# A memory-augmented block on one core: the late queries and keys move from the memory rows' softmax to the token rows' softmax

## The chip, the cores and the metric

One core of a Trainium2 chip runs the whole program. The metric is the device time of one execution in microseconds (us); of several runs the median is given.

## The reference

Input `x` is 2048 tokens of 512 numbers in bf16. The first half is a recurrent attention with 32 heads of 128, over 64 segments of 32 tokens, with 8 memory rows that go from segment to segment:

```
xn = layernorm(x); mem = mem0
for s in 64 segments:
    h = concat(mem (8 rows), xn[segment s] (32 rows))        # 40 rows
    q, k, v = h @ Wq, h @ Wk, h @ Wv
    scores = q k^T / sqrt(128); a token row sees the memory rows and the tokens up to itself,
                                a memory row sees all 40
    o = softmax(scores) v, then @ Wo
    mem = o[:8];  out[segment s] = o[8:]
h  = x + out
h2 = h + w2(gelu(w1 layernorm(layernorm(h)) + b1)) + b2
```

The mask is `(idx_q < 8) | (idx_q >= idx_k)`: a memory row (query index below 8) sees all 40 keys; a token sees the memory rows and the tokens up to and with itself. The memory rows of one segment are input to the projections of the next, so the segments form a chain.

## The kernel before

All weights lie in SBUF. The loop has 64 steps, one per segment (`s`); four segments form a block (`bk = s // 4`, `sg = s % 4`). The 40 rows of a segment are split into two packs. The first holds 24 tokens ("early" tokens) and the 8 memory rows and is projected in its own step, because of the memory rows (`hT`). The last 8 tokens of a segment ("late" tokens) depend on no memory row; those of four segments make 32 rows (`hB`) that are projected a block ahead: K in a step with sg = 0, Q with sg = 1, V with sg = 2 (parts `F0`, `F1`). With sg = 3 the same place holds the output product of the late rows (`wo_B`).

PE works in tiles of 128 rows by 32 columns: four matmuls side by side, 512 columns each, make a *pass unit*, and a projection of 16 heads has four (one per quarter of the 512 inputs). A unit that uses the same quarter of the same tokens as the unit just before it keeps the loaded tokens and issues no weight loads (`matmul_kept`, L604).

The parts of a step, in PE's order:
- `Q0`, `Q1`, `K0`, `K1` (L871): projections of 16 heads each. The result is copied by ACT or DVE (`kq`), transposed by DVE (L912) into `QT`, `KALL`, and the memory rows' queries are copied on into `ZC` by POOL (`ZCm`, L926).
- `SC0`, `SC1` (L1036): scores of the memory rows, for 16 heads each. `ZC` holds, per head, the 8 memory queries and the 8 late queries (`ZCb`, L933, POOL), so the stationary 32 columns are two heads with 16 rows each, and the scores are two groups of 64 keys (32 of the own pack and 32 of late keys, of which a mask leaves 8). The softmax `sc_softmax` is a maximum (L1044), two exponentials with sums (L1053, ACT), two reciprocals (L1058), two products (L1061) and one transposition to `PTC` (L1063, DVE).
- `V0`, `V1`: projections of V (`VS`).
- `PV0`, `PV1` (L1074, L1079): `PTC` times V, in tiles of 64 rows by 128 columns; L1079 takes the late values `VBD`. Out come the memory rows (`OTm`) and the late rows (`OTB`).
- `PVA` (L1142): the same for the token rows of the step before, from `BD`.
- `WO` (L1170): output product, eight units. Its result is transposed (`TT`, L1182) and summed into the next step's memory rows (`hTm`, L1176).
- `SA` (L1104): scores of the 24 token rows, 32 matmuls of 32 columns (32 keys; the late tokens' queries are not among them). Its softmax: L1114, L1115, L1116, L1117, L1118, the product `PA` (L1125), the transposition `PTA` (L1127), and four copies into the block form `BD` (L1131, POOL), which the next step's PVA reads.

The order on PE is written out by hand in four lists, one for each sg (`ORDERS`); an entry `('F1', 1, 2)` takes the part's units from 1 up to but not including 2. The other engines' orders come from a planner in the program: each operation has a duration and a planned time (`PLAN`, us), operations that more than one engine can do (`either`) go where they end first or where `HOME` says, and gaps are filled. After that `align()` counts PE's instructions in blocks of 256 and pads the pass units with up to 8 spare weight loads each (L869), so that a step of sg = 0, 1, 2, 3 begins at instruction 0, 64, 128, 192 of a block; if the stream is less than 24 instructions past that place nothing is done, else it is filled up to the next one:

```
owed = (PHASE[seg % 4] - at) % FETCH_N       # PHASE = (0, 64, 128, 192), FETCH_N = 256
if owed > FETCH_N - SLIP: owed = 0           # SLIP = 24
o.pad[0] = min(owed, PADS)                   # PADS = 8
```

After the loop comes a feed-forward phase (L1569, L1576) that the change leaves as it is.

## Time and profile before

| | us |
|---|---|
| median of 3 runs (lowest to highest) | 819.95 (818.89 to 820.13) |
| span of the profiled execution, first to last instruction | 817.0 |
| steps 1 to 3 begin at | 51.12, 63.03, 73.42 |
| steps 5 to 56 (94.74 to 637.48) | 542.74 |
| loop's end and feed-forward phase, from 730.31 | 86.7 |

The span leaves out 2.95 us of the median: what lies ahead of the first and behind the last instruction, and the difference between executions. In rows of a timeline the first number is the start in us from the span's start, the second the length; matmuls overlap, so PE is read from start to start. In rows of groups the last part is: busy time, mean ns of one | idle time of the engine just before them and what ended it.

### The profile page before, as it was taken

The page shows a single profiled execution, that of the slowest core. Times are in us where ns is not written, and L with a number is a line of the kernel's source. Part 1 is how long each engine was busy: PE and PEld are TensorE (multiplying, and loading weights), DVE is VectorE, ACT ScalarE, POOL GpSimd, SP SyncE. Part 2 cuts the span into 40 slices and gives each one's busy share as a digit, 9 for nine tenths or more (in the row PEclk, how much of TensorE's full clock was granted, in tenths as well). Part 3 has the DMA queues.
Part 4 walks back from the last instruction along what each step waited for, and adds up shares of the span by engine and source line. Part 5 has one row for each costly group of instructions (what it writes and reads, how often), then busy time and mean ns, then how long its engine had stood idle before and what let it go on. Part 6 is the DMA issues. An engine that isn't in the chain of part 4 may idle for free.

```text
span 817.0 us, 43604 instructions
## 1 busy us (share of the span) xinstructions
PE 780.8 (96%) x19317; PEld 426.6 (52%) x18878; DVE 622.1 (76%) x2008; ACT 529.6 (65%) x1522; POOL 351.2 (43%) x886
## 2 busy tenths in 40 slices
PE   3788999999999999999999999999999999999998
PEld 1345555555556555555555556555555555544443
DVE  3268797989898989898989898888899887833211
ACT  2446677767776767777777777767676766643442
POOL 5023334545454545454545454545463535367200
PEclk9989999999999999999999999999999999999999
DMA  8950010111101010101010201010112131265200
GB/s 341 391 173 16 4 25 15 30 30 27 32 21 39 17 42 14 45 10 43 10 49 10 49 10 49 10 49 3 49 29 62 37 91 26 76 173 147 55 26 26
DMA packets 65449, 48.03 MB, mean 59 GB/s; under 512 B 29028, under 2 KB 61676, under 8 KB 65260
## 3 DMA queue, kind: packets, MB, share of 16 engines
q1 hardware_dynamic: 64928, 44.98, 18.5%
q8 instruction: 150, 2.46, 1.3%
q14 instruction: 39, 0.32, 0.1%
q10 hardware_dynamic: 332, 0.27, 0.1%
HBM read 31.08 MB, written 8.13 MB: 48 GB/s over the span
## 4 chain that ended last, share of the span: by engine, by line
PE 77%; DVE 8%; ACT 7%; SPq 5%; issue 1%; DMA 1%; DVEq 0%
PE ps L871 33%; PE ps L1170 15%; PE quad L1576 6%; PE ps L604 5%; PE ps L1569 5%; ACT EC L1053 4%; PE quad L1074 4%; ACT kq L889 3%; DVE KALL L912 3%; SPq L791 2%; PE ps L1209 2%; DVE PC L1061 2%; SPq L774 2%; PE ps L1104 2%; DVE nmc L1044 2%; PE quad L1142 2%
## 5 line engine op out<-in xcount | busy, mean ns | idle before, releaser
L871 PE MATMUL ps<-WQ,hT 128*32 128x512 bf16 x2048 | 159.9, 384 | 5.7 <-DVE hT L1176 5.6
L1170 PE MATMUL ps<-WO,OT 128*32 128x256 bf16 x4224 | 141.3, 274 | 1.4 <-DMA WO<-in_A_Wo_dram 0.9
L871 PE MATMUL ps<-WV,hT 128*32 128x512 bf16 x1780 | 142.5, 379 | 0.0
L890 ACT ACTIVATE kq<-ps 128x512 bf16<-128x512 f32 x146 | 87.2, 597 | 66.1 <-PE ps L871 65.8
L1125 POOL TENSOR_TENSOR PA<-SA,rsa 128x256 bf16<-128x256 f32 x64 | 39.8, 621 | 187.4 <-DVE rsa L1118 174.5
L889 ACT CAST kq<-ps 128x512 bf16<-128x512 f32 x160 | 93.4, 583 | 37.8 <-PE ps L871 37.8
L1170 PEld LDWEIGHTS ps<-WO,OT 128*32 128x32 bf16 x4224 | 96.4, 96 | 24.4 <-issue 2.9
L1131 POOL COPY BD<-PTA 32x192 bf16<-32x192 bf16 x256 | 96.4, 376 | 16.7 <-DVE PTA L1127 0.9
L1061 DVE SCALAR_TENSOR_TENSOR PC<-EC,rsc,even 128x128 bf16<-128x128 f32 x256 | 94.6, 371 | 6.6
L871 PE MATMUL ps<-WK,hT 128*32 128x512 bf16 x1292 | 93.6, 379 | 0.0
L871 PEld LDWEIGHTS ps<-WQ,hT 128*32 128x32 bf16 x2048 | 60.5, 96 | 59.8 <-issue 19.4
L912 DVE STREAM_TRANSPOSE KALL<-kq 128x256 f32<-128x256 f32 x160 | 70.5, 441 | 22.9 <-ACT kq L889 20.6
L1053 ACT ACTIVATE EC<-quad,nmc 128x64 f32<-128x64 f32 x252 | 77.1, 311 | 7.6 <-DVE nmc L1044 0.9
L604 PE MATMUL ps<-WK,hT 128*32 128x512 bf16 x756 | 76.5, 382 | 0.0
L889 ACT CAST VS<-ps 128x512 bf16<-128x512 f32 x126 | 73.8, 586 | 0.9
L889 ACT CAST OT<-quad 128x128 bf16<-128x128 f32 (+1 forms) x193 | 65.2, 358 | 10.7 <-PE quad L1079 7.7
L912 DVE STREAM_TRANSPOSE QT<-kq 128x256 f32<-128x256 f32 x128 | 57.0, 446 | 18.7 <-ACT kq L890 18.6
L871 PEld LDWEIGHTS ps<-WV,hT 128*32 128x32 bf16 x1780 | 51.9, 96 | 33.7 <-issue 1.4
L1572 ACT ACTIVATE WQ<-ps,b1t 128x512 bf16<-128x512 f32 x42 | 28.9, 688 | 51.9 <-PE ps L1569 51.9
L1116 ACT ACTIVATE SA<-SA 128x256 f32<-128x256 f32 x64 | 26.7, 417 | 55.0 <-DVE SA L1115 52.7
L871 PEld LDWEIGHTS ps<-WK,hT 128*32 128x32 bf16 x1292 | 38.5, 97 | 44.5 <-issue 19.6
L1222 POOL TENSOR_TENSOR opT<-TTB,TTS 32x64 bf16<-32x64 f32 x128 | 40.3, 315 | 32.4 <-DVE opT L1176 23.2
(160 smaller groups left out, 1485.9 us busy)
## 6 DMA issues: line engine op xcount, KB each, us to landing
WV<-in_A_Wv_dram SPq DMA_DIRECT2D x4, 1024.0 KB, 10.4
WK<-in_A_Wk_dram SPq DMA_DIRECT2D x4, 1024.0 KB, 18.0
WQ<-in_A_Wq_dram SPq DMA_DIRECT2D x4, 1024.0 KB, 18.9
WO<-in_A_Wo_dram SPq DMA_DIRECT2D x16, 256.0 KB, 7.8
v_last<-VSB SPq DMA_DIRECT2D x60, 64.0 KB, 3.1
VBD<-v_last SPq DMA_DIRECT2D x60, 64.0 KB, 2.9
h_mid<-xr SPq DMA_DIRECT2D x16, 128.0 KB, 1.9
WQ<-h_mid SPq DMA_DIRECT2D x4, 512.0 KB, 4.3
```

What stands on the lines that cost most here:

```text
L604: return e.add_instruction(mybir.InstMatmult(name="I-%d" % (4000000 + _kept[0]), engine=mybir.EngineType.PE, start_tensor_calc=start, stop ...
L871: ins = e.matmul(o, l, m, start=(k == 0), stop=(k == DC - 1), tile_position=(0, 32 * j), skip_group_check=True)
L889: return {"act": (lambda e: e.copy(out, src), t_act(n, ps_)), "dve": (lambda e: e.tensor_copy(out, src), 0.155 + 1.0e-3 * n * fast)}
L890: return {"act": (lambda e: e.mul(out, src, scale_), t_act(n, ps_)), "dve": (lambda e: e.tensor_scalar(out, src, scale_, None, ALU.mult), ...
L912: S.op("dve", lambda e: e.transpose(out, src), reads=[("kq", i)], writes=[key], dur=t_dve(256) + 0.02)
L1053: return e.activation(EC[:, r, sl, :], o[:, sl, :], ACTF.Exp, bias=nmc[:, r, sl:sl + 1], accum_out=smc[:, r, sl:sl + 1])
L1061: S.op("dve", lambda e, sl=sl, xc=xc: e.scalar_tensor_tensor(PC[:, r, :, :, sl], xc, rsc[:, r, sl:sl + 1], ev, ALU.mult, ALU.mult), reads= ...
L1131: S.narrow(S.op("pool", lambda e, j=j, rows=rows: e.tensor_copy(BD[rows, par, :, j, :, :], PTA[rows, :, 0:NA, :]), reads=["PTA"], writes=[ ...
L1170: ins = e.matmul(ps[bank][32 * j:32 * j + 32, 0:256], lhs(slot(h)), wo_cols(h, b), start=(k == 0), stop=(k == 15), tile_position=(0, 32 * ...
L1222: return e.tensor_tensor(o[32 * q:32 * q + 32, c:c + 2], x, y, ALU.add)
L1569: ins = e.matmul(ps[bank][:, 0:SBT], W1[:, cc, fc * P:(fc + 1) * P], hnT_of(k)[:, cc, :], start=(cc == 0), stop=(cc == DC - 1))
L1576: S.op("pe", lambda e: e.matmul(quad[:, t, :], gT_of(k, fc)[:, t * P:(t + 1) * P], W2[:, fc, :], start=(fc == 0), stop=(fc == FC - 1)), re ...
```

## The change

The softmax of the memory rows keeps only the memory queries: `ZC` has 8 rows per head, the stationary 32 columns are four heads, and one group of 64 scores per SC remains. One maximum, one exponential, one reciprocal, one product per SC. The mask moves from `[128]` to `[64]` columns; PV has 16 columns per matmul and 64 for the late values.

The late queries go to SA: `ql_fill` writes them over the memory rows of `QT` after `ZCm` has been copied out, and `kl_fill` puts the segment's 8 late keys beside the 32 of the pack in `KALL` (`LK = 40` keys). SA then has 32 query rows and 40 keys. Its softmax grows from 8 x 32 to 8 x 40 numbers. A second product `PL` puts the late keys' weights into a fifth slice of `PA`; after the transposition a new product `BDL` (with a mask `maskD`) makes the block form for the late values. PVA gets 32 rows per head in place of 24 and four matmuls more, with `VBD`. `OTB` is copied out of PVA's result and no longer out of PV's. `ZCb` (`qb_fill`) is gone.

Besides, `ORDERS`, `PLAN`, `HOME` are new, and some durations that the planner uses; a hop from an engine to PE counts 0.06 more. The core of the diff:

```diff
-ORDERS = ((('Q0', 0, 1), ('K0', 0, 1), ('Q0', 1, 2), ('K0', 1, 2), ('Q0', 2, 3), ('Q1', 0, 1), ('Q0', 3, 4), ('K0', 2, 4), ('Q1', 1, 4), ('K1', 0, 4), ('SC0', 0, 99), ('V0', 0, 1), ('V1', 0, 1), ('V0', 1, 4), ('F1', 0, 1), ('SC1', 0, 99), ('V1', 1, 2), ('F0', 0, 1), ('V1', 2, 3), ('F1', 1, 2), ('V1', 3, 4), ('PV0', 0, 99), ('PVA', 0, 99), ('F1', 2, 3), ('WO', 0, 2), ('PV1', 0, 99), ('WO', 2, 8), ('F1', 3, 4), ('SA', 0, 99), ('F0', 1, 4)),
+ORDERS = ((('K0', 0, 2), ('Q0', 0, 2), ('K0', 2, 3), ('Q0', 2, 4), ('Q1', 0, 1), ('K0', 3, 4), ('Q1', 1, 4), ('K1', 0, 4), ('SC0', 0, 99), ('F0', 0, 1), ('V0', 0, 2), ('V1', 0, 1), ('V0', 2, 4), ('F1', 0, 1), ('SC1', 0, 99), ('V1', 1, 3), ('F1', 1, 2), ('V1', 3, 4), ('PV0', 0, 99), ('PVA', 0, 99), ('F1', 2, 3), ('WO', 0, 2), ('PV1', 0, 99), ('WO', 2, 8), ('F1', 3, 4), ('SA', 0, 99), ('F0', 1, 4)),
+          (('Q0', 0, 2), ('K0', 0, 1), ('Q0', 2, 4), ('K0', 1, 2), ('Q1', 0, 1), ('K0', 2, 4), ('Q1', 1, 4), ('K1', 0, 4), ('V0', 0, 1), ('SC0', 0, 99), ('V0', 1, 3), ('V1', 0, 1), ('V0', 3, 4), ('F1', 0, 1), ('SC1', 0, 99), ('V1', 1, 4), ('F1', 1, 3), ('PV0', 0, 99), ('PVA', 0, 99), ('F1', 3, 4), ('PV1', 0, 99), ('WO', 0, 8), ('F0', 0, 1), ('SA', 0, 99), ('F0', 1, 4)),
...
-        "SP0": (-1.81, -1.81, -1.52, -1.65),
+        "SP0": (-0.304, -1.667, 0.575, 1.283),
...
-        return HOP[p.eng]
+        return HOP[p.eng] + (0.06 if o.eng == "pe" else 0.0)
...
-        def qb_fill(s, after=()):
-            ...
-            S.op("pool", lambda e: e.tensor_copy(dst, src), reads=[("QTB", bk % 2, q) for q in range(2)], writes=[("ZCb", par)], dur=0.41, after=after)
+        def ql_fill(s):
+            ...
+            S.either({"act": (lambda e: e.copy(dst, src), 0.34), "dve": (lambda e: e.tensor_copy(dst, src), 0.24), "pool": (lambda e: e.tensor_copy(dst, src), 0.34)},
+                     reads=[("QTB", bk % 2, q) for q in range(2)], writes=[("QL", 0), ("QT", 0), ("QT", 1)])
+        def kl_fill(s):
+            ...
+                     reads=[("KB", bk % 2, q) for q in range(2)], writes=[("KL", s % 2)])
...
+            S.op("act", lambda e: e.activation(EC[:, r, :], o, ACTF.Exp, bias=nmc[:, r:r + 1], accum_out=smc[:, r:r + 1]),
+                 reads=[("nmc", r), bkey], writes=[("EC", r), ("smc", r)], dur=0.42)
+            S.op("dve", lambda e: e.reciprocal(rsc[:, r:r + 1], smc[:, r:r + 1]), reads=[("smc", r)], writes=[("rsc", r)], dur=0.16)
...
-            S.op("pe", f, reads=[("QT", 0), ("QT", 1), ("KA", par, 0), ("KA", par, 1)], writes=[("ps", bank)], dur=0.25, mode=MC, ni=64)
+            S.op("pe", f, reads=[("QT", 0), ("QT", 1), ("KA", par, 0), ("KA", par, 1), ("KL", par)],
+                 writes=[("ps", bank)], dur=0.26, mode=MC, ni=64)
...
+            S.either({k: (..., w) for k, w in (("dve", 0.24), ("pool", 0.32))}, ["SA", "rsa"], ["PL"], after=after)
...
-                S.narrow(S.op("pool", lambda e, j=j, rows=rows: e.tensor_copy(BD[rows, par, :, j, :, :], PTA[rows, :, 0:NA, :]), ...
+                S.narrow(S.op("pool", lambda e, j=j, rows=rows: e.tensor_copy(words(BD[rows, par, :, j, :, :]), words(PTA[rows, 0:4])), ...
+            S.either({k: ((lambda e: e.tensor_tensor(BDL[:, par], src, msk, ALU.mult)), w) for k, w in (("dve", 0.3), ("pool", 0.45))},
+                     reads=["PTA", "maskD"], writes=[("BDL", par)])
...
+                for r in range(2):
+                    for t in range(2):
+                        ...
+                        ins = e.matmul(o, VBD[rows, bk % 2, sg, r, :], BDL[rows, s % 2, r], start=False, stop=True, tile_position=(64 * t, 0), skip_group_check=True)
-            S.op("pe", f, reads=[("VS", par, 0), ("VS", par, 1)] + [("BD", s % 2, j) for j in range(4)], writes=AQ, dur=0.29, mode=MH, ni=32)
+            S.op("pe", f, reads=[("VS", par, 0), ("VS", par, 1), ("BDL", s % 2)] + [("BD", s % 2, j) for j in range(4)] + [("VBD", bk % 2, j) for j in range(4)],
+                 writes=AQ, dur=0.27, mode=MH, ni=40)
...
+                    ql_fill(s)
+                    kl_fill(s)
                     sa_mm(s, bank_of[name])
```

The other two lists of `ORDERS` are changed in the same way: with sg = 2 the units are Q0 0-1, K0 0, Q0 2, K0 1-2, Q0 3, K0 3, Q1, K1, SC0, V0 0-1, V1 0, V0 2-3, F1 0, SC1, F1 1, V1 1-3, PV0, PVA, F1 2-3, WO 0, PV1, WO 1-7, F0 0-2, SA, F0 3; with sg = 3 they are Q0 0, K0 0, Q0 1, K0 1, Q0 2-3, Q1 0, K0 2-3, Q1 1-3, K1, V0 0, SC0, V0 1-3, V1 0, F0 0, SC1, V1 1-3, F0 1-2, PV0, PVA, F0 3, PV1, WO, SA, F1.

## The prediction

> **What bounds the kernel now.** First the page: which engine is full.

> ```profile
> span 817.0 us, 43604 instructions
> ...
> PE 780.8 (96%) x19317; PEld 426.6 (52%) x18878; DVE 622.1 (76%) x2008; ACT 529.6 (65%) x1522; POOL 351.2 (43%) x886
> ...
> q8 instruction: 150, 2.46, 1.3%
> ```

> PE is busy for 96% of the span. "Busy" counts overlapping matmuls, so it does not show small gaps. Then the busy time by stretch: the middle of the loop (steps 5 to 56), a step with s%4 = 0 and one with s%4 = 2; after the stretch's length come the busy times of PE, its weight loads, DVE, ACT and POOL.

> ```profile
> 94.74:637.48 542.74, 539.01 (x15189) 304.04 (x14506) 481.76 (x1597) 392.96 (x1183) 259.00 (x661) 1.00 0.12 30
> ```
> ```profile
> 376.19:387.31 11.12, 10.45 (x296) 5.81 (x284) 9.38 (x32) 7.42 (x22) 5.42 (x13) 1.00 0.02 3
> ...
> 397.73:408.04 10.31, 10.28 (x297) 5.73 (x285) 9.66 (x33) 7.50 (x22) 5.66 (x15) 1.00 0.02 5
> ```

> 542.74 us over 52 steps is 10.44 us a step; a smooth step takes 10.31 us and this s%4 = 0 step 11.12. The clock is granted in full (1.00). What PE's 10.31 us consist of, the timeline of PE in one step shows, with one row of the chain in order of time for the price of a pass.

> ```profile
> 401.19 0.30 PE L1036 MATMUL quad<-KALL,ZC 128*32 128x64 bf16 x16
> 401.31 0.40 PE L871 MATMUL ps<-WV,hT 128*32 128x512 bf16 x4
> ...
> 403.62 0.40 PE L871 MATMUL ps<-WV,hB 128*32 128x512 bf16 x4
> 404.05 0.27 PE L1074 MATMUL quad<-PTC,VS 64*128 64x32 bf16 x8
> 404.14 0.23 PE L1079 MATMUL quad<-PTC,VBD 64*128 64x128 bf16 x2
> 404.20 0.37 PE L1142 MATMUL quad<-BD,VS 64*128 64x48 bf16 x16
> 404.51 0.40 PE L871 MATMUL ps<-WV,hB 128*32 128x512 bf16 x4
> 404.73 0.62 PE L1170 MATMUL ps<-WO,OT 128*32 128x256 bf16 x16
> 405.29 0.27 PE L1074 MATMUL quad<-PTC,VS 64*128 64x32 bf16 x8
> 405.40 0.22 PE L1079 MATMUL quad<-PTC,VBD 64*128 64x128 bf16 x2
> 405.55 1.50 PE L1170 MATMUL ps<-WO,OT 128*32 128x256 bf16 x48
> 406.87 0.42 PE L1104 MATMUL ps<-KALL,QT 128*32 128x32 bf16 x32
> 407.12 1.06 PE L871 MATMUL ps<-WV,hB 128*32 128x512 bf16 x16
> 408.04 0.41 PE L871 MATMUL ps<-WQ,hT 128*32 128x512 bf16 x4
> ```
> ```profile
> 398.78 1.73 PE ps L871 x32
> ```

> Read start to start. A pass unit of four matmuls takes 1.73/8 = 0.216 us. Forty units (24 of Q, K, V, 8 of the block's work, 8 of WO) are 8.65 us of the 10.31; the rest is small matmuls, changes of PE's tile mode, and waits. Two waits stand out. From 403.62 to PV0 at 404.05 are 0.43 us, of which 0.216 is the unit; going into PV1 the same change of mode costs 405.29 - 404.73 - 2 x 0.22 = 0.12; so PE waits about 0.10 us for PV0. And from 407.12 to 408.04 are 0.92 us for four units (0.865): about 0.06 of waiting for the next step's memory rows. So PE's own work is the bound and the recurrence is nearly as long. PV0 waits for the memory rows' softmax:

> ```profile
> 403.59 0.31 DVE L1063 STREAM_TRANSPOSE PTC<-PC 128x128 f32<-128x128 f32 x1
> ```

> It ends at 403.90, 2.71 us after SC0 began at 401.19, and PV0 follows 0.15 us later.

> **The change part by part.** *The memory rows' softmax is halved* (64 scores a row in place of 2 x 64).

> ```profile
> L1061 DVE SCALAR_TENSOR_TENSOR PC<-EC,rsc,even 128x128 bf16<-128x128 f32 x256 | 94.6, 371 | 6.6
> ...
> L1053 ACT ACTIVATE EC<-quad,nmc 128x64 f32<-128x64 f32 x252 | 77.1, 311 | 7.6 <-DVE nmc L1044 0.9
> ...
> L1053 ACT ACTIVATION_READ_ACCUMULATOR EC<-quad,nmc 128x1 f32 x252 | 49.8, 198 | 0.0
> ...
> L1063 DVE STREAM_TRANSPOSE PTC<-PC 128x128 f32<-128x128 f32 x128 | 39.9, 312 | 4.3
> ...
> L1044 DVE TENSOR_REDUCE nmc<-quad 128x2 f32<-128x128 f32 x126 | 36.8, 292 | 0.6 <-PE quad L1036 0.6
> L1058 DVE RECIPROCAL rsc<-smc 128x1 f32<-128x1 f32 x256 | 35.0, 137 | 0.0
> ...
> L1114 DVE TENSOR_REDUCE nma<-ps 128x8 f32<-128x256 f32 x64 | 27.2, 425 | 2.9 <-PE ps L1104 0.9
> ```

> Per SC, one multiplication (0.371) and one reciprocal (0.137) leave the DVE sequence that ends in PTC, 0.51 us. The reduction and the transposition lose 64 elements; from 128 to 256 a reduction grows by (425 - 292)/128 = 1.04 ns an element, so 0.067 each. Together about 0.64 us off the 2.71. ACT loses one exponential and its read per SC, 2 x 0.51 = 1.0 us a step, but with 7.50 of 10.31 us busy it was no bound. The new part orders spend some of this: in three of four orders PV0 comes 10 units after SC0 instead of 11 (0.216), and PV1 6 or 7 units after SC1 instead of 8. At least 0.2 us is left over, so I take the 0.10 us before PV0 as gone. What is late next is PE itself: it executes in order.

> *PE's own matmuls.* Four pairs of 32 columns (404.05 to 404.14) take 0.023 us a pair. PVA's eight pairs of 48 columns take 0.31 us less the change back (405.40 to 405.55 is 0.15, less 0.055 for the pair: 0.10), 0.21, or 0.026 a pair. Below 48 columns the number of columns hardly counts, so PV at 16 columns saves nothing; were it proportional, it would be 0.05 per PV, and I keep that end for the range. The late values' pair goes from 128 columns (0.055, 404.14 to 404.20) to 64: -0.027, twice a step. PVA gets 64 columns in place of 48 (8 x 0.001) and two more pairs of 64 (2 x 0.028): +0.065. SA's 32 matmuls go from 32 to 40 columns: eight groups of four now take 0.25 us, 0.031 a group, and SC's groups with 64 columns take 0.12/4 = 0.030 (401.19 to 401.31), so nothing. Changes of mode stay four a step. Net: -0.054 + 0.065 = +0.01 us a step.

> *Late queries and keys in SA.* Three DVE operations and one exponential grow by 64 elements, 4 x 0.067 = 0.27 us in the token rows' tail; PL (a product) and BDL (a product) are new, and QL and KL (copies) take the place of ZCb.

> ```profile
> L1131 POOL COPY BD<-PTA 32x192 bf16<-32x192 bf16 x256 | 96.4, 376 | 16.7 <-DVE PTA L1127 0.9
> ...
> L1125 POOL TENSOR_TENSOR PA<-SA,rsa 128x256 bf16<-128x256 f32 x64 | 39.8, 621 | 187.4 <-DVE rsa L1118 174.5 <-DVE hT L1176 12.0 <-ACT kq L890 0.9
> ...
> L926 POOL COPY ZC<-QT 128x128 bf16<-128x128 bf16 x126 | 37.0, 293 | 22.5 <-DVE QT L912 19.1
> ...
> L933 POOL COPY ZC<-QTB 128x256 bf16<-128x256 bf16 x64 | 25.5, 399 | 32.0 <-DVE QTB L912 20.8 <-DVE KALL L912 11.1
> ```
> ```profile
> 400.95 0.27 DVE L1127 STREAM_TRANSPOSE PTA<-PA 128x128 f32<-128x128 f32 x1
> ...
> 402.05 1.70 POOL L1131 COPY BD<-PTA 32x192 bf16<-32x192 bf16 x4
> ```

> QL and KL cost about 0.29 each (the 128-element copy), 0.40 goes with ZCb. SA gets to wait for both, and behind SA on PE stand one to four pass units and the next step's first projections. QL itself waits for the ZCm copies, the second of which POOL ends before the BD copies begin at 402.05; SA comes at 406.87, so it is hidden; uncovered it would cost 0.3 us a step. PL lies between 0.29 and 0.62; PL and the wider SA operations delay PTA by about 0.6 us. BD started only after the second ZCm copy, with PTA ready at 401.22, 0.8 us before, so this too is covered. The four BD copies move 128 words instead of 192 elements, 0.29 to 0.376 each. BDL, 0.29 to 0.62, is new between PTA and PVA: on DVE it runs beside BD, on POOL behind it. BD ended at 403.75 and PVA began at 404.20, so 0.45 us is in hand, of which the earlier PV0 takes 0.1 to 0.3. I take no wait; this is the thinnest cover of the change. OTB's copy moves behind PVA and has until the next steps; its banks are needed again by the next SC0 and SC1, some 7 us on. No DMA is added or taken away; SP's order follows the planned times as before.

> *PE's instruction stream.* Each 256 instructions come as one 16 KB block (150 blocks, 2.46 MB, on the page). Now 15189 + 14506 instructions in 52 steps are 571 a step, with PE's waits 576; four steps make 2304 = 9 x 256, which align() holds to by a few spare weight loads. In s%4 = 0 a block ends inside SA, and there PE stands still:

> ```profile
> 385.66 0.24 PE L1104 MATMUL ps<-KALL,QT 128*32 128x32 bf16 x12
> 386.54 0.30 PE L1104 MATMUL ps<-KALL,QT 128*32 128x32 bf16 x20 [0.64 <-issue]
> ```
> ```profile
> PEld ps L1104 <- issue: 3.0, 9, 0.7
> ```

> Twelve matmuls take 0.09 us; the thirteenth came 0.8 us late, with nothing waited for. Over the run it is 3.0 us in nine steps. The change adds 8 instructions to each PVA. By the new orders 4, 1, 3 and 4 units of a step reuse the loaded tokens of the unit before, against 4 in each now; each such unit saves 4 loads, so 16 more. That is 48 more in four steps, too many for 2304, and align() then fills to the next phase with some 220 spare loads, eight per pass: ten blocks in four steps, and in one step of four a block lasts 16 passes x 0.216 = 3.5 us, about what the block that ends in SA lasts today (from just before PV0 to SA, 3.3 us). Bounds: nothing (the loads lie under the matmuls, and most blocks today end without a stall), or 0.3 to 0.8 us for each of three dense blocks. Taken: one small stall more, 0.1 us per four steps.

> [...]

> *Elsewhere.* In steps 1 to 3, where a block's work is missing, PE waits longer for PV0:

> ```profile
> 68.06 0.83 PE L871 MATMUL ps<-WV,hT 128*32 128x512 bf16 x12
> 69.35 0.27 PE L1074 MATMUL quad<-PTC,VS 64*128 64x32 bf16 x8 [0.46 <-ACT EC L1053]
> ```

> 1.29 us for three units and the change of mode (0.77): 0.5 us, all of it inside the 0.64. The start (weights landing) and the second phase are untouched: 0.

> **The sum.** Steps 4 to 59: 56 x (-0.10 + 0.01) = -5.0. Steps 1 to 3: -1.5. Steps 60 to 62: -0.3. PV1's wait (0.02 of its 0.12 beyond the change of mode): -0.6, half of it taken, if the new orders use it. Blocks: 14 x 0.1 = +1.4. Together -6.0; with 817.0 this is a span of 811.0. The median of the runs, 819.95, stands 2.95 above the span, which gives 813.9; I say 814. A measurement of this kernel tells apart about 0.2%, 1.6 us. The likeliest case's own range is 809 to 818.

> **The rivals.** *More gain* (806): the wait for memory rows shrinks as well (0.06 a step, 3.4 us, since DVE and ACT have less queued) and the new stream ends no block inside SA (3.0 us), and the +1.4 falls away. For it: DVE loses about 1.3 us a step of old work. Against: DVE already waits for PE before that step's end, and SA keeps nearly its place in the stream.

> *Slower by fetching* (826): three dense blocks per four steps stall 0.45 us each, 14 x 1.35 = 19, against a gain of 7.4: +12 at worst; with 1.0 us per four steps, +6.6. It decides from 0.5 us per four steps on. For it: the row of SA, in a block just as long. Against: even that block stalled in only nine of some fifteen steps.

> *Slower by PVA* (826): BDL lands on POOL behind the BD copies and ends after PVA's place. At 0.2 us a step, 59 x 0.2 = 12, against 6: +6. It decides from 0.1 us beyond the cover. For it: 0.45 us in hand against up to 0.62. Against: DVE can take BDL, and BD gets shorter.

> *No difference* (819 to 820): the orders' shifts use up the freed softmax time, or stalls of 0.4 us per four steps eat the gain.

> **How the numbers follow.** Forecast 0.46, more gain 0.17, no difference 0.07, fetching 0.17, PVA 0.13. Faster by over 0.2%: 0.63; within: 0.07; slower: 0.30. The range, 803 to 829, takes in PV at a cost by columns (-5.6 more) at its lower end and both slow rivals at its upper.

> **What would show it.** Right: PTC ends some 2.1 us after SC0, the gap into PV0 falls to 0.12 us, steps with s%4 = 2 take about 10.2 us, and about 165 blocks of instructions are fetched. Wrong: idle time of PE put down to "issue" outside SA, a wait of PVA's weight loads for POOL or DVE, SC0 held up by the ZCm copy behind PL on POOL, or a step that is not shorter though PV0 no longer waits.

## The result and the profile after

The changed kernel takes 841.92 us (median of 4 runs, 838.48 to 844.58); the kernel before, on the same chip, 819.42 us (4 runs, 817.12 to 820.13). The ratio is 1.027, 95% interval 1.024 to 1.030. The forecast was 814 us, 803 to 829: wrong in sign and outside its range. The profiled execution took 841.63 us for a span of 839.9; beside the 817.0 of before these are 22.9 us more.

The page of the changed kernel (engine, busy us, share, instructions; then the queue that brings instructions: packets, MB, share):

```profile
PE 787.0 (94%) x19573; PEld 468.2 (56%) x22135; DVE 592.6 (71%) x1815; ACT 522.7 (62%) x1306; POOL 342.7 (41%) x958
...
q8 instruction: 164, 2.69, 1.4%
```

DVE lost 30 us of work and ACT 7, what the halved softmax saves less what the new operations cost; the weight loads (PEld) grew from 18878 to 22135, and 164 blocks of instructions came in place of 150. Now the busy time by stretch, for steps 1 to 3 and 4 to 55, first of before, then of after:

```profile
51.12:83.92 32.80, 28.52 (x789) 17.14 (x928) 25.41 (x85) 19.41 (x60) 12.17 (x32) 0.95 0.09 21
83.92:626.92 543.00, 539.08 (x15184) 304.58 (x14576) 481.88 (x1597) 392.74 (x1182) 256.85 (x656) 1.00 0.11 29
```
```profile
51.15:84.65 33.50, 28.60 (x801) 17.87 (x925) 22.80 (x72) 20.02 (x55) 11.80 (x35) 0.95 0.10 22
84.65:647.19 562.54, 544.34 (x15392) 342.27 (x17625) 458.54 (x1439) 387.32 (x1002) 254.17 (x734) 1.00 0.12 28
```

Of the 22.9 us, 19.5 lie in steps 4 to 55. Four neighbouring steps of after, with s%4 = 1, 2, 3 and 0:

```profile
397.00:407.43 10.43, 10.32 (x296) 6.29 (x295) 8.75 (x29) 7.94 (x21) 4.88 (x15) 1.00 0.05 16
407.43:418.55 11.12, 10.72 (x296) 7.90 (x499) 8.91 (x29) 7.20 (x19) 6.53 (x20) 1.00 0.02 5
418.55:429.62 11.07, 10.39 (x300) 6.20 (x284) 9.39 (x29) 7.62 (x20) 3.87 (x12) 1.00 0.36 86
429.62:439.95 10.33, 10.33 (x301) 5.86 (x277) 8.29 (x28) 7.03 (x18) 4.77 (x14) 1.00 0.02 5
```

Two of the four take 11.1 us. The step with s%4 = 2 holds 499 weight loads where the others hold 277 to 295: there `align()` put its spare loads, 214 of them. The timeline of PE shows where the time goes, in that step and at the end of the next:

```profile
414.89 0.26 PE L1063 MATMUL quad<-PTC,VS 64*128 64x16 bf16 x8
415.00 0.19 PE L1067 MATMUL quad<-PTC,VBD 64*128 64x64 bf16 x2
415.12 0.29 PE L1174 MATMUL ps<-WO,OT 128*32 128x256 bf16 x3
415.81 1.69 PE L1174 MATMUL ps<-WO,OT 128*32 128x256 bf16 x53 [0.40 <-issue]
...
427.89 0.63 PE L1213 MATMUL ps<-WO,OTB 128*32 128x512 bf16 x8
429.19 0.61 PE L1213 MATMUL ps<-WO,OTB 128*32 128x512 bf16 x8 [0.68 <-issue]
```

Three matmuls of WO, then nothing for 0.6 us, then the other 53, with no producer named. From 427.89 to 429.19 are 1.30 us for two units (0.43): 0.87 lost. Both are the picture that the prediction showed inside SA, and SA's own stall is gone. The waits list them by line (total us, times, longest):

```profile
PEld ps L1213 <- issue: 16.7, 16, 1.4
PEld ps L1174 <- issue: 12.1, 20, 1.6
```

What moves meanwhile is seen in the busy share of the DMA engines, here the stretch from 411 to 419 us in 40 slices of 0.2 us:

```profile
DMA  0000000000003000000000000000040000000000
GB/s 0 0 0 0 0 0 0 0 0 0 0 0 82 0 0 0 0 0 0 0 0 0 0 0 0 0 0 0 0 82 0 0 0 0 0 0 0 0 0 8
...
q8 instruction: 2, 0.03, 1.8%
```

Two blocks of instructions and hardly anything else: 82 GB/s for 0.2 us are 16 KB, and so are 2.69 MB for 164 packets. By the packet records the first began at 413.43 and had landed at 414.39; PE went on at 415.81, 1.42 us after it. PE's records (matmuls, loads and waits) come to 257 a packet, here as in before. In steps 4 to 55 of after two neighbouring ones begin over 0.4 us apart 29 times, and 27 of these places, as all four of before, lie a multiple of 256 records apart. Counted so, the instruction at 415.81 is the first of a new block of 256, and the first of the block ahead of it was executed at 411.73. So the block's successor began to come 1.70 us after PE entered the block and took 0.97, and PE had run through all 256 instructions in 3.4 us.

The same count over steps 4 to 55 of all fourteen kernels told of here gives this. Of 1,659 blocks, none was entered earlier than 1.19 us after its landing (1.19 is the least in after, 1.26 in before). At 278 block ends PE stood still for more than 0.2 us; it went on 1.41 us (median; four in five between 1.26 and 1.57) after the next block had landed (1.43 at the 37 ends in before and after). A fetch took 1.1 us (0.9 to 1.7), and the time from entering a block to the start of the next fetch was 1.0 us (median) where PE did not stand still and 1.6 where it did (0.8 and 1.6 in before and after). That PE stands still for want of the block is inferred from these places and times, as no record names a cause. By the medians a block needed, as an estimate, some 3.5 us (1.0 + 1.1 + 1.4), and 4.1 where the fetch started late. Of 205 blocks with less than 3.5 us of work 136 ended in such a stall (29 of 52 in after), of 513 with 3.5 to 4.2 us 121, of 941 longer ones 21.

### The profile page after: what moved, and what is told of

It is laid out like the page before. It is cut to its first block, busy times and chain, and to the rows that moved or that the text cites. A ratio compares the mean times of both kernels' runs of the same rounds, so it can differ in the third digit from the quotient of the medians.

```text
span 839.9 us, 46983 instructions
## 1 busy us (share of the span) xinstructions
PE 787.0 (94%) x19573; PEld 468.2 (56%) x22135; DVE 592.6 (71%) x1815; ACT 522.7 (62%) x1306; POOL 342.7 (41%) x958
## 3 DMA queue, kind: packets, MB, share of 16 engines
q8 instruction: 164, 2.69, 1.4%
## 4 chain that ended last, share of the span: by engine, by line
PE 88%; SPq 5%; issue 3%; DVE 2%; DMA 1%; POOL 0%; ACT 0%; DVEq 0%; POOLq 0%
PE ps L859 44%; PE ps L1174 15%; PE quad L1575 6%; PE ps L603 5%; PE ps L1568 4%; PE ps L1213 4%; PE quad L1063 3%; SPq L779 2%; SPq L762 2%; PE quad L1035 2%; PE quad L1135 2%; PE ps L1089 2%; PE ps L1368 1%; DMA WO<-in_A_Wo_dram 1%; PE quad L1067 1%
## 5 line engine op out<-in xcount | busy, mean ns | idle before, releaser
L859 PE MATMUL ps<-WQ,hT 128*32 128x512 bf16 x1800 | 144.3, 382 | 6.4 <-DVE hT L1180 5.2
L859 PE MATMUL ps<-WK,hT 128*32 128x512 bf16 x1544 | 121.3, 381 | 1.9 <-DVE hT L1180 1.6
L1174 PEld LDWEIGHTS ps<-WO,OT 128*32 128x32 bf16 x4224 | 106.6, 97 | 22.7 <-issue 12.1
L1120 POOL COPY BD<-PTA 32x128 f32<-32x128 f32 x256 | 76.7, 300 | 23.6 <-DVE PTA L1116 5.9
L1114 POOL TENSOR_TENSOR PA<-SA,rsa 128x64 bf16<-128x64 f32 x64 | 19.1, 298 | 161.2 <-DVE rsa L1104 142.4
L859 PEld LDWEIGHTS ps<-WK,hT 128*32 128x32 bf16 x1544 | 47.7, 96 | 44.8 <-issue 20.9
L857 PEld LDWEIGHTS <-hT 128*32 128x32 bf16 x3007 | 54.3, 96 | 28.3 <-issue 11.3
L923 POOL COPY ZC<-QT 128x128 bf16<-128x128 bf16 x126 | 36.6, 290 | 56.6 <-DVE QT L900 54.4
L1186 DVE STREAM_TRANSPOSE TT<-ps 128x256 f32<-128x256 f32 x66 | 29.7, 450 | 42.5 <-PE ps L1174 41.3
L1102 ACT ACTIVATE SA<-SA 128x320 f32<-128x320 f32 x64 | 30.1, 470 | 46.1 <-DVE SA L1101 46.1
## 6 DMA issues: line engine op xcount, KB each, us to landing
WV<-in_A_Wv_dram SPq DMA_DIRECT2D x4, 1024.0 KB, 10.7
```

Of the source, the lines that this page charges most:

```text
L857: e.ldweights(l, tile_position=(0, 32 * j))
L859: ins = e.matmul(o, l, m, start=(k == 0), stop=(k == DC - 1), tile_position=(0, 32 * j), skip_group_check=True)
L923: S.either({"act": (lambda e: e.copy(dst, src), 0.31), "dve": (lambda e: e.tensor_copy(dst, src), 0.25), "pool": (lambda e: e.tensor_copy( ...
L1120: S.narrow(S.op("pool", lambda e, j=j, rows=rows: e.tensor_copy(words(BD[rows, par, :, j, :, :]), words(PTA[rows, 0:4])), reads=["PTA"], w ...
L1174: ins = e.matmul(ps[bank][32 * j:32 * j + 32, 0:256], lhs(slot(h)), wo_cols(h, b), start=(k == 0), stop=(k == 15), tile_position=(0, 32 * ...
```

## The experiments

Each of the twelve has "before" run on its own chip, at 819.65 to 820.49 us, and its ratio is to that.

| run | us | ratio (95%) | steps 4 to 55, us |
|---|---|---|---|
| before | 819.42 | 1 | 543.00 |
| after | 841.92 | 1.024 to 1.030 | 562.54 |
| e1 no spare loads | 825.69 | 1.005 to 1.008 | 549.59 |
| e2 before with 256 spare loads | 833.91 | 1.014 to 1.019 | 555.18 |
| e3 spare loads thinner | 836.41 | 1.017 to 1.023 | 557.31 |
| e4 nine blocks in four steps | 825.10 | 1.004 to 1.008 | 551.20 |
| e5 e4 moved by 96 | 833.92 | 1.015 to 1.023 | 554.72 |
| e6 e4 moved by 80 | 823.90 | 1.004 to 1.008 | 551.42 |
| e7 e4 drifting | 825.84 | one run | 552.47 |
| e8 before drifting | 827.88 | one run | 551.10 |
| e9 e4 moved by 232 | 816.79 | 0.994 to 0.997 | 543.05 |
| e10 before moved by 240 | 831.95 | 1.012 to 1.016 | 556.11 |
| e11 e1 with one wait | 826.04 | one run | 551.94 |
| e12 e9 stretched | 819.36 | 0.997 to 1.000 | 544.18 |

**Is it the spare loads?** e1 takes them out of the changed kernel:

```diff
-PHASE = (0, 64, 128, 192)
+PHASE = ()
```

> The changed kernel without spare weight loads: PE's program is not realigned every step, the rest is as changed (about 2346 instructions per four steps in place of 2560, the block ends drift through the step). Theory F (the spare loads pack 256 instructions into about 3.4 us of PE time, the next block lands too late, PE stands still 0.7 to 1.1 us in WO and wo_B): the two stalls per four steps go, 14 x 1.6 = 22 us less, 818 to 823 us; what drift costs could add up to 3. Rival S (the new part orders and planned times themselves leave PE waiting): unchanged, 840 to 844 us.

16.2 of the 22.5 us go; 6 stay, 2.7 more than expected. Steps without a stall in the stretch list of e1 (s%4 = 0, 1, 2):

```profile
296.03:306.52 10.49, 10.49 (x298) 6.58 (x282) 8.63 (x29) 7.03 (x18) 4.77 (x14) 1.00 0.02 6
306.52:316.97 10.45, 10.38 (x301) 6.38 (x293) 8.80 (x29) 7.93 (x21) 4.94 (x15) 1.00 0.06 16
316.97:327.37 10.40, 10.40 (x298) 6.01 (x286) 8.90 (x29) 7.24 (x19) 6.44 (x19) 1.00 0.02 4
```

Others last up to 11.6: in e1 the block ends wander through the steps, and where they come to lie badly PE stands still there too. e2 puts such loads into the kernel before, where nothing else is changed:

```diff
                 if owed > FETCH_N - SLIP:
                     owed = 0
+                owed += 256 * (seg % 4 == 2)
```

> The kernel before with 256 spare weight loads, eight per pass unit, in every step with s%4 = 2 and nothing else changed (2560 instructions per four steps, as in the changed kernel). Theory F: two dense blocks per four steps, 0.7 to 1.7 us, 14 times: 829 to 843 us, with idle time of PE put down to issue behind them. Rival S: the loads lie under the matmuls, 819 to 821 us.

14 us more, as theory F had it; the rival's 819 to 821 is out. A step with the loads and the one after it:

```profile
405.42:416.00 10.58, 10.56 (x296) 7.42 (x539) 9.72 (x33) 7.53 (x22) 5.56 (x15) 1.00 0.02 6
416.00:426.40 10.40, 10.38 (x296) 5.70 (x286) 9.12 (x31) 7.51 (x23) 4.41 (x12) 1.00 0.36 89
```

These two are among the mild ones (the median of the steps with the loads is 11.12). So the loads are sufficient, and in after they are most of the loss.

**Number of blocks or density?** e3 spreads the same 214 loads thinner:

```diff
-FETCH_AT, PADS, SLIP = 65, 8, 24
+FETCH_AT, PADS, SLIP = 65, 4, 24
```

> The changed kernel with the same 214 spare loads per four steps, but at most four per pass unit, so that they spread over steps with s%4 = 2 and 3; 12 instructions per unit make a block last 256/12 x 0.216 = 4.6 us of pure passes in place of 3.5. Theory F by density: most of the stall goes, 820 to 827 us. Rival C (every further block fetched costs the same, wherever it lies): 840 to 844 us, as many blocks are fetched.

836.41: only 5.5 us less, so neither was right. The fetches are as many (164). Two steps now share the loads and both are long:

```profile
402.79:413.97 11.18, 10.70 (x297) 7.09 (x421) 8.85 (x28) 7.22 (x19) 6.48 (x19) 1.00 0.01 4
413.97:425.20 11.23, 10.36 (x300) 6.75 (x360) 9.77 (x29) 7.52 (x20) 3.90 (x12) 1.00 0.35 86
```

My 4.6 us a block was for plain passes. A block that also holds PV, PVA, WO or SA (64 instructions in 0.25 us) is shorter: in e3's records the short ones last 3.4 to 4.2 us. Of the 28 that end in a stall 11 last 3.4 us, below the estimate of 3.5; 13 last 3.7 to 3.8, and there the fetch mostly began late, 1.8 us (median) after PE had entered the block.

**Can the change be had in nine blocks?** e4 alters the four orders so that more pass units reuse loaded tokens (4, 7, 7 and 5 in place of 4, 1, 3 and 4), 2299 instructions in four steps in place of 2560, and each step begins with K0. One of the four lists:

```diff
-          (('Q0', 0, 2), ('K0', 0, 1), ('Q0', 2, 4), ('K0', 1, 2), ('Q1', 0, 1), ('K0', 2, 4), ('Q1', 1, 4), ('K1', 0, 4), ...
-           ('F1', 3, 4), ('PV1', 0, 99), ('WO', 0, 8), ('F0', 0, 1), ('SA', 0, 99), ('F0', 1, 4)),
+          (('K0', 0, 1), ('Q0', 0, 1), ('K0', 1, 2), ('Q0', 1, 3), ('K0', 2, 3), ('Q0', 3, 4), ('K0', 3, 4), ('Q1', 0, 4), ('K1', 0, 4), ...
+           ('F1', 3, 4), ('PV1', 0, 99), ('WO', 0, 8), ('F0', 0, 3), ('SA', 0, 99), ('F0', 3, 4)),
```

> The changed kernel with its part orders altered so that a step begins with K0 (whose bank DVE frees, so the first weight load waits for DVE's memory rows alone and not for ACT too) and more pass units reuse the loaded tokens (4, 7, 7 and 5 in place of 4, 1, 3 and 4): 2299 instructions per four steps, nine blocks, five spare loads. Theory F with W (the second wait at the step's start costs 0.08 us in three of four steps): no stall, 56 x about 10.26 to 10.33: 813 to 819 us. F without W: 818 to 821. Rival S: 838 to 844.

825.10, a miss by 6 us: only 150 blocks are fetched, no spare loads to speak of, and PE still stands still in two of four steps (s%4 = 0, 1, 2, 3):

```profile
379.05:389.87 10.82, 10.47 (x298) 6.69 (x284) 8.49 (x28) 7.14 (x18) 4.87 (x14) 1.00 0.01 4
389.87:400.39 10.52, 10.46 (x300) 5.48 (x264) 8.83 (x29) 7.54 (x19) 4.74 (x15) 1.00 0.07 17
400.39:410.76 10.37, 10.37 (x296) 5.42 (x273) 9.10 (x29) 7.56 (x20) 6.80 (x20) 1.00 0.02 4
410.76:421.75 10.99, 10.37 (x299) 5.80 (x281) 9.27 (x29) 7.53 (x20) 3.82 (x12) 1.00 0.35 87
```

So the number of blocks isn't all; the place where they end must count. The *phase* of a step is the place in a block of 256 at which the step begins. e5, e6 and e9 keep e4's orders and move the phases alone:

```diff
-PHASE = (0, 64, 128, 192)
+PHASE = (96, 160, 224, 32)      # e5
+PHASE = (80, 144, 208, 16)      # e6
+PHASE = (232, 40, 104, 168)     # e9
```

> The kernel of the run e4_aligned with the same orders and the same number of instructions; only the place in each step where a block of 256 ends is moved by 96 instructions (the four target phases 96, 160, 224, 32 in place of 0, 64, 128, 192). Theory P (what decides is where the block ends fall: one that ends just ahead of PV0, in PVA or around SA has its successor late; the drifting run e1_no_spare had steps without a stall at about these phases): the stalls of e4_aligned go, 811 to 818 us. Rival N (only the number of blocks and of spare loads counts): as e4_aligned, 823 to 827 us.

> As e5_aligned_96, moved by 80 instructions. Theory P: close to it, 811 to 820 us, with a stall in steps with s%4 = 3 if their edge (a stall at phase 13, none at 17 in e1_no_spare) is met. Rival N: 823 to 827 us.

The map that I had read from e1 failed: e5 was slower by 9 us than e4 and not faster, as its stalls had only moved (the waits of e5; L1086 is SA and L1171 is WO there):

```profile
PE ps L1086 <- issue: 7.4, 8, 1.4
PE ps L1171 <- issue: 6.4, 9, 1.1
```

e6, at 823.90, came where the rival N had put it and not where theory P had. But with e5 the rival N fails too, as the same instructions, 150 or 151 blocks, take 825, 834 and 824 us. Two drifting runs, planned together with e5 and e6, were to give a map of the places.

```diff
-                owed = (PHASE[seg % 4] - at) % FETCH_N
-                if owed > FETCH_N - SLIP:
-                    owed = 0
+                owed = (118 - at) % FETCH_N if seg == 1 else 0
```

> The orders of e4_aligned without realignment, its first step set so that the phase of s%4 = 0 steps drifts from about 120 down to 50, five a block. Theory P: the steps change length with the phase, 10.25 to 10.45 us where no stall falls and 10.7 to 11.3 where one does, each kind in a run of neighbouring blocks. Rival N: no pattern by phase.

> The kernel before without realignment (2292 instructions per four steps in place of 2304, so the phase drifts by 12 a block). Theory P: the kernel before has stalls too where the phase is bad, so it loses 3 to 12 us against itself: 822 to 832 us. Rival N: no spare loads, no more blocks: 818 to 821 us.

(e8 is before with `PHASE = ()`.) In e7 the steps with s%4 = 0 last 10.21 to 10.23 us in six neighbouring blocks of phases 70 to 95 and 10.50 to 10.94 at phases 100 to 115; those with s%4 = 3 last 10.23 at 50 and 10.8 to 11.3 from 5 to 35. So there is a pattern, though not without exceptions. e8, at 827.88, suggests, from one run, that the kernel before depends on its alignment as well: without it, it loses 8 us with fewer blocks (148).

> The kernel of e4_aligned with the target phases 232, 40, 104, 168, chosen from the step lengths that the drifting runs e1_no_spare and e8_before_drift showed by phase (steps near 230, 48, 105 and 160 had no stall in them). Theory P (the place of a block's end decides): 21 of the 22 us of stall are gone and no others come, 14 x about 41.3 us per four steps: 811 to 818 us. If the new orders have moved the bad places, as e5_aligned_96 suggests they can, one stall per four steps is left: 820 to 826. Rival N: 823 to 827.

> The kernel before with its target phases moved to 240, 48, 112, 176, by the map of e8_before_drift. Theory P: the stall inside SA in steps with s%4 = 0 goes (3.5 us), unless phase 47 in s%4 = 1 meets the stall that 37 had and 49 had not: 815 to 818 us, 824 if it does. Rival N: 819 to 820 us.

e9, 816.79, is the fastest of all (0.996 of before, 95% interval 0.994 to 0.997). Its steps (s%4 = 0 to 3), and its stretches for steps 1 to 3 and 4 to 55:

```profile
372.95:383.74 10.79, 10.61 (x301) 6.64 (x284) 9.02 (x29) 7.13 (x18) 4.83 (x14) 1.00 0.05 16
383.74:394.11 10.37, 10.37 (x302) 5.48 (x266) 8.69 (x29) 7.54 (x19) 4.88 (x15) 1.00 0.06 17
394.11:404.44 10.33, 10.33 (x296) 5.43 (x273) 9.06 (x29) 7.57 (x20) 6.75 (x20) 1.00 0.02 4
404.44:414.69 10.25, 10.25 (x302) 5.80 (x283) 8.58 (x28) 7.55 (x20) 3.91 (x12) 1.00 0.34 80
```
```profile
50.51:80.77 30.26, 26.75 (x801) 16.25 (x898) 22.71 (x72) 19.85 (x55) 11.70 (x35) 1.00 0.10 23
80.77:623.82 543.05, 539.70 (x15393) 299.18 (x14327) 457.89 (x1440) 387.89 (x1002) 256.86 (x733) 1.00 0.12 29
```

The total lies in the range of theory P, but not all stalls are gone: three of the four steps have none in the median; the one with s%4 = 0 loses 0.34 us inside SA. Steps 4 to 55 take what they take in before (543.05 against 543.00): what the others gain, this one loses. The profiled span is 2.6 us shorter (814.4): 3.2 us are won ahead of step 4, in steps 1 to 3 (30.26 against 32.80, at a clock of 1.00 in place of 0.95; at 1.00, in e10, before's take 31.4) and in the start (50.51 against 51.12), and 0.5 are lost behind step 55. So no run shows steps 4 to 55 faster than before's. e10 moved before's ends and made it slower by 11.5 us: at phase 47 the steps with s%4 = 1 stall in most blocks, which the expectation had named, but the price it gave (824) was too low, and the stall of s%4 = 0 did not go.

**Is it the length of the block in time?** e12 takes e9 and moves two units in steps with s%4 = 0, so that the block from PV to SA holds more plain passes:

```diff
-('F1', 1, 2), ('PV0', 0, 99), ('PVA', 0, 99), ('F1', 2, 3), ... ('F0', 1, 2), ('SA', 0, 99), ('F0', 2, 4)
+('PV0', 0, 99), ('PVA', 0, 99), ('F1', 1, 3), ... ('F0', 1, 3), ('SA', 0, 99), ('F0', 3, 4)
```

> e9_aligned_232 with two pass units moved in steps with s%4 = 0 alone, F1's second from ahead of PV0 to behind PVA and F0's third from behind SA to ahead of it, so that the block which runs there from PV to SA holds 16 instructions of plain passes (0.43 us) in place of as many of SA (0.06 us). Theory D (a block of 256 needs lag + fetch + 1.4 us, 3.5 to 3.9 us here, and this one holds 3.4 us of work): the idle time inside SA falls from 0.34 us (SA 0.56 in place of 0.22) to under 0.1. PV0 then has a unit less ahead of it and may wait 0.1 us, and the next step's PVA may wait up to 0.08 for the later SA: 813 to 817 us in all. Rival: the stall belongs to the place of SA and stays, 817 to 820.

In e9, the timeline of that place, and then in e12:

```profile
382.75 0.27 PE L1086 MATMUL ps<-KALL,QT 128*32 128x40 bf16 x16
383.19 0.28 PE L1086 MATMUL ps<-KALL,QT 128*32 128x40 bf16 x16 [0.18 <-issue]
383.31 0.60 PE L856 MATMUL ps<-WK,hB 128*32 128x512 bf16 x8
```
```profile
384.57 0.82 PE L856 MATMUL ps<-WK,hB 128*32 128x512 bf16 x12
385.22 0.41 PE L1086 MATMUL ps<-KALL,QT 128*32 128x40 bf16 x32
385.44 0.41 PE L856 MATMUL ps<-WK,hB 128*32 128x512 bf16 x4
```

SA takes 0.22 us start to start again in the median step (0.56 in e9; means 0.31 and 0.58, so a few stalls are left). The block's work grew from 3.33 to 3.82 us, its end still lies inside SA, and a stall of over 0.2 us is left in 5 of 13 blocks, where e9 has 10. So the stall went with the length of the block, at the same part of the step. The time did not follow, 819.36 in place of 816.79, inside the rival's range. Of the 3.2 us between the two profiled spans, 1.6 lie ahead of step 1, where the profiles of these kernels differ anyway (50.5 to 52.8 us), and 1.1 in steps 4 to 55. There PVA, now a unit earlier, waits 0.13 us behind PV, which I had put at 0.1, and the next step grew from 10.37 to 10.56. For that I had put 0.08 at PVA, but the wait is at SC0, which starts 0.17 us late (0.01 in e9): in the step from 385.73, the queries `QT` are ready at 388.55, but their copy `ZCm` runs on POOL at 389.14, behind `PL` and `PA`, and SC0's first load comes at 389.55. In e9 the stall ahead of this step seems to have covered that wait. It is a sign of error that the prediction had named, though in after SC0 waits only 0.01 us on average.

**Where did the gain of the unstalled steps go?** In after, the steps without a stall were hardly shorter than those of before (10.33 and 10.50 us with s%4 = 0 and 1, against 10.50 and 10.40), though PV0's wait was gone. The end of each step waits for the memory rows (`hT`), and where the first weight load has to wait for ACT as well (the bank of Q0 is also that of F1) it comes later. e11 is e1 with K0 first in three of four orders:

```diff
-          (('Q0', 0, 2), ('K0', 0, 1), ('Q0', 2, 4), ...
+          (('K0', 0, 1), ('Q0', 0, 4), ...
```

> e1_no_spare with one edit: in steps with s%4 = 1, 2 and 3 the first pass unit is K0 in place of Q0, so the first weight load of the step waits for DVE alone and not for ACT and DVE. Theory W (a second wait on that load costs 0.08 us): the idle time at the end of unstalled steps falls by 0.08 us in three of four steps, the first weight load starts 0.07 us after the memory rows in place of 0.15; the total 3 us lower, 820 to 825 us, as stalls shift with the phase. Rival: the 0.15 us has another cause and stays.

The timelines of e1 and e11 at the same place, the start of a step with s%4 = 2:

```profile
316.32 0.50 DVE L1180 TENSOR_TENSOR hT<-TT 64x32 bf16<-64x32 f32 x2
316.94 0.15 PEld L859 LDWEIGHTS ps<-WQ,hT 128*32 128x32 bf16 x8 [0.54 <-issue]
316.97 0.61 PE L859 MATMUL ps<-WQ,hT 128*32 128x512 bf16 x8
```
```profile
314.84 0.52 DVE L1180 TENSOR_TENSOR hT<-TT 64x32 bf16<-64x32 f32 x2
315.42 0.10 PEld L859 LDWEIGHTS ps<-WK,hT 128*32 128x32 bf16 x4 [0.47 <-DVE hT L1180]
315.42 0.40 PE L859 MATMUL ps<-WK,hT 128*32 128x512 bf16 x4
```

The first matmul comes 0.06 us after `hT` has ended in place of 0.15. In e1 it is 0.15 in all three kinds of step, whether ACT's last copy had ended 0.2, 0.9 or 2.7 us before, so it is not ACT that comes late. Worked out from the starts in the timeline, the idle time at the end of a step (medians) falls from 0.14, 0.28 and 0.16 us to 0.05, 0.20 and 0.07 in steps with s%4 = 0, 1, 2 and stays at 0.04 with 3. So the second wait costs 0.08 to 0.09. The total did not show it (826.04 in one run, above the range expected); with eleven instructions less per four steps the block ends lie elsewhere, and the stalls that steps with s%4 = 3 have here (median 10.86 us, 10.35 in e1) may have eaten it.

## Why the prediction was wrong

The step that failed is the term for instruction blocks; the gain was mis-sized as well. Here are the prediction's own steps, with means over steps 4 to 54 from starts in PE's timeline.

- *PV0's wait, -0.10 a step*: right. The time into PV0 fell from 0.22 to 0.12 us. PTC ends 2.02 us after SC0 began (433.08 to 435.10 in one step), 2.1 was said.
- *PE's own matmuls, +0.01*: near. PVA takes 0.40 in place of 0.305 (+0.10, not +0.065), both PV together 0.05 less: +0.04 or so. PV0's four pairs, now of 16 columns, take 0.11 us (414.89 to 415.00), where 32 columns took 0.09.
- *The covers* of QL, PL, BDL and the later PTA held: no wait of PVA for POOL or DVE of any size is in after's list of waits (0.4 us in two places). The rival "slower by PVA" is out for this kernel; e12 shows that a unit less ahead of PVA brings a wait of 0.13 us.
- *Steps 1 to 3, -1.5*: they stalled as well (1.6 us once, inside WO), 33.50 in place of 32.80. In e9 they take 30.26; before's need 31.4 at the full clock (e10, whose blocks end elsewhere), so 1.2.
- *Instruction blocks, +0.1 us per four steps*: this step failed. That align() would fill with about 220 loads (214 came), in one step of four, with dense blocks, and about 165 fetches (164) was all foreseen. The price was not: in steps with s%4 = 2 the stall costs 0.72 us and at the end of those with 3 0.89, against 0.22 that the old stall in SA took off. Net 1.4 us per four steps in place of 0.1, 13 times: 18 of the 19.5 us by which steps 4 to 55 grew. Even the rival "slower by fetching" had put three blocks at 0.45 us each; they were two at 0.8. Its worst case, 12 us slower, was half of what came.
- The argument for the low price was the row of SA: a block of 3.3 us that stalled in only nine of some fifteen steps, and a dense block of 3.5 us that would be "about" as long. Both lengths were wrong. Counted back by 256 instructions from the thirteenth matmul of SA at 386.54, the block in before begins with this row, two units ahead of PV0:

```profile
381.87 0.40 PE L871 MATMUL ps<-WK,hB 128*32 128x512 bf16 x4
```

So it holds 3.86 us of work, not 3.3, and it gets through when its fetch starts early (0.8 to 1.0 us after it was entered) and stalls or only just passes when it starts 1.55 us or later. The 3.5 us for a dense block counted pure passes; with SC, PV and PVA inside it was 3.1 to 3.4, 0.5 to 0.8 less than the block it was likened to, and 23 of 24 such blocks stalled.
- *The gain, -0.09 a step*: without stalls about half of it came, see below. PV0's 0.10 us partly reappeared at the end of the step, where in three orders the first load waits for ACT and DVE (0.08 to 0.09, shown by e11). This wait was in no part of the prediction, though one order of before had it.

What the change is worth without stalls is read from the best four steps in a row. They take 41.52 us in before, 41.35 in e6 and 41.27 in e11. (The short steps with s%4 = 0 in e6 and e7, 10.20 to 10.23 us, are each followed by a long one, 10.56 to 10.61.) This is 0.04 to 0.06 us a step, about half of what the prediction gave the change, and no run holds it over the whole loop. In e9 the stall in one step of four takes it back.

What stays open is why the time from PE's first instruction of a block to the start of the next fetch varies so much, from 0.8 us before it to 3.0 after it (0.11 to 2.13 after it in before and after). The place in the step seems to have a part in it (over 1.5 us in 41 of 93 blocks entered in PVA, in 251 of 1,566 others), yet at one place both kinds occur. No run changed this alone.

## What to carry to other kernels

Count instructions as well as microseconds on an engine whose stream is long and dense: lay the ends of the instruction blocks over the timeline, and see which of them are short (here 136 of 205 with under 3.5 us of work ended in a stall). Padding for alignment is not free merely because it lies under other work: here 214 loads in four steps cost 16.2 us (after against e1). They took up places in the blocks around them, which held 3.1 to 3.4 us of work. And when a chain of parts is reordered, look at how many engines the first instruction after the critical result must wait for (here a second one cost 0.08 to 0.09 us, e11).
